# A two-layer threshold-attention and squared-ReLU kernel: the order of its first loads, of its PSUM banks, and of its side work at the seams

## The chip, the cores and the metric

The kernel runs on one core of one Trainium2 chip. The metric is the device time of one execution in microseconds: the median of 3 runs of the kernel before is 1271.97 us (1270.42 to 1272.17). Five engines work beside each other: TensorE (PE, with PEld for its weight loads), VectorE (DVE), ScalarE (ACT), GpSimd (POOL) and SyncE (SP), which here only issues DMAs. Each runs its own instructions in the order in which they were written, and waits for the others by semaphores.

## The reference

All arithmetic is float32. The weights of the two layers come in as 64-bit floats and are converted on the chip.

```python
# q, k, v: (8, 8, 576, 64); w_in: (512, 2048); w_out: (2048, 512)
scores = scale * np.matmul(q, k.transpose(0, 1, 3, 2))
thresh = np.max(scores, axis=-1, keepdims=True) - tau
scores = np.where(scores >= thresh, scores, -1000000000.0)
attn = np.exp(scores - np.max(scores, axis=-1, keepdims=True))
attn = attn / (np.sum(attn, axis=-1, keepdims=True) + 1e-09)
x = np.matmul(attn, v)          # -> (4608 tokens, 512), heads side by side
h = np.maximum(x @ w_in, 0.0)
out = (h * h) @ w_out
```

## The kernel before

The program has three stages, one behind the other. **Attention** takes pairs of heads; `load_q` and `load_k` bring queries and keys, `turn` transposes them on PE against the identity `ident` into PSUM and evicts them scaled by `qscale` (made from `tau`), `scores` multiplies, DVE and ACT do the softmax, `values` multiplies by v. Its PSUM is one tile `sc` of six banks and a pool `pt` of two. At the start, `keep_busy` runs transposes of the identity on PE while the first loads are under way. `rn` is a tile that holds the last 64 queries of both heads and the last 64 keys' chunk; `load_k` fills it by small loads.

The two layers are matrix products done by Strassen's scheme in Winograd's form, twice nested: seven outer products m, in the order `OUTER` = 1, 2, 6, 7, 4, 5, 3, each made of seven inner products k, in the order 1, 6, 7, 5, 2, 4, 3. The **hidden layer** (first layer) runs over all tokens first. The **output layer** (second layer) then runs over nine steps n of 512 tokens, 49 products of eight matmuls each per step.

`inner` is one outer product m. Its banks are called X, Y, Z, W here. PE makes X (k = 1), Y (k = 6), Z (k = 7), W (k = 5), then adds onto X (k = 2), Z (k = 4) and W (k = 3). ACT copies X out as p1 (`copy`, the **first copy**, line 813); DVE adds u2 = Y + p1 and u3 = Z + u2, and `final` takes each of the four results out (line 126). Z may be added to again only when u3 has read it. Between these, `tick(0)` to `tick(6)` call `also`, which issues side work.

The **side work** of the output layer makes the operands of products that come later. `inner_sums(n, m)` makes, for the next m, its operands k = 5, 6 and 3 on POOL and its operand k = 7 on DVE. The latter is `sum_v`: ACT copies one input into a PSUM tile `c` of the pool `b` (two buffers, line 857), then DVE subtracts (line 123). `outer_sums` makes operands of another m, all in that manner. `spread` deals the list of side work over the seven ticks. With the four items of `inner_sums` alone, the fourth (k = 7) falls on tick 6. The lists of i = 4 and 5 (m = 4 and 5) have ten items in steps 0 to 7, of which two fall on tick 6; that of i = 6 (m = 3) has eight. In step 0, i = 0, 1 and 2 have longer lists, too.

```python
for w in work[n * at // 7 : n * (at + 1) // 7]:
    w()
```

The order of every engine's instructions is the order of these calls: the whole is scheduled by hand.

Of the kernel before, what the change touches and what calls it, by code (L numbers as in the profile page):

```python
# [10 lines left out]
FP32 = mybir.dt.float32  # L11
I32 = mybir.dt.int32
U32 = mybir.dt.uint32
ALU = mybir.AluOpType
# [34 lines left out]
def kernel(  # L49
# [54 lines left out]
    sb, cv = Region(arena, 0, X_AT[0]), Region(arena, X_AT[0], ARENA)  # L104

    ident = const.tile([P, P], FP32, name="ident")
    make_identity(nc, ident)

    tau_c = const.tile([P, 1], FP32, name="tau_c")

# [14 lines left out]
    def plus(e, out, x, y):  # L125
        e.tensor_tensor(out=out, in0=x, in1=y, op=ALU.add)  # L126
# [184 lines left out]
    def load_k(i):  # L311
        b, hp = pairs[i]
        h = 2 * hp
        kn = sb.tile([P, FULL, P], FP32, tag="kn", bufs=2, name="kn")
        rn = sb.tile([P, P], FP32, tag="rn", bufs=2, name="rn")
        loaded[i, 1], loaded[i, 2] = kn, rn
        for j in range(2):
            queue = nc.scalar if i == 0 and j == 0 else nc.sync
            keys = k[b, h + j, :, :].rearrange("(p c) d -> p c d", c=CH)
            for e in range(2):  # L320
                yield queue.dma_start(
                    out=kn[ds(e * HALF, HALF), :, ds(j * D, D)],
                    in_=keys[:, ds(e * FULL, FULL), :],
                )
            if i == 0 and j == 0:
                wide = bass.AP(tensor=tau.tensor, offset=tau.offset, ap=[[0, P], [1, 1]])
                nc.scalar.dma_start(out=tau_c[:, :], in_=wide)
            yield queue.dma_start(out=rn[REST:P, ds(j * D, D)], in_=keys[:, CH - 1, :])
        yield nc.sync.dma_start(
            out=rn[0:REST, :].rearrange("p (j d) -> p j d", j=2),  # L330
            in_=q[b, h : h + 2, MAIN:S, :].rearrange("j p d -> p j d"),
        )
# [81 lines left out]
    def turn(i, which, spots, other=None):  # L414

        while any(x[0:2] == (i, which) for x in wanted):
            ahead(1)
        nat, to = loaded.pop((i, which)), places(i)
        of = [nat[:, t, :] for t in range(FULL)] + ([loaded.pop((i, 2))] if which else [])
        for t, x in enumerate(of):  # L420
            for r, (spot, at) in enumerate(spots):
                rows = ds(r * HALF, HALF)
                made = nc.tensor.transpose(spot[:, ts(t, HALF)], x[rows, :], ident[rows, rows])  # L423
                touch("turns", made, at, BANK)
        half, kind = FULL * HALF, "turnedk" if which else "turnedq"

        def scaled(to, spot):
            touch(kind, nc.scalar.activation(out=to, in_=spot[0], func=AF.Identity, scale=qscale[:, :]), spot[1], BANK, i)

        def then():  # L430
            part = lambda r, x, n: (spots[r][0][:, ds(x, n)], spots[r][1])
            if which:
                for r, n in ((0, half), (1, half + REST)):
                    spot = part(r, 0, n)
                    copy_by = other if r and other else nc.scalar.copy
                    touch(kind, copy_by(to[1][:, ds(r * half, n)], spot[0]), spot[1], BANK, i)
                scaled(to[2], part(0, half, REST))
                ask_ahead(i, 1)
            else:
                for r in range(2):  # L440
                    scaled(to[0][:, ds(r * half, half)], part(r, 0, half))
                ask_ahead(i, 0)

        return then
# [330 lines left out]
        for name in BEGIN_WITH.get(p) or (CONVERTING if converts(p) else PLAIN):  # L775
            step(name.rstrip("-"), p - name.count("-"))

    def inner(product, copy, temp, bank, final, tick):

        X = bank()
        product(X, 1, False)
        p1 = temp("p1")
        copy(p1, X)
        tick(0)
        Y = bank()
        product(Y, 6, False)
        u2 = temp("u2")  # L790
        plus(nc.vector, u2, Y, p1)
        tick(1)
        Z = bank()
        product(Z, 7, False)
        u3 = temp("u3")
        plus(nc.vector, u3, Z, u2)
        tick(2)
        W = bank()
        product(W, 5, False)
        final((1, 1), W, u3)  # L800
        tick(3)
        product(X, 2, True)
        final((0, 0), X, None)
        tick(4)
        product(Z, 4, True)
        final((1, 0), Z, u2)
        tick(5)
        product(W, 3, True)
        final((0, 1), W, u2)
        tick(6)  # L810
# [151 lines left out]

    hid = Region(arena, 0, 26 * BANK)
    squares, clock = deque(), {"n": 0}
    def hidden_bank():
        return banks.tile([P, BANK], FP32, tag="b", bufs=6, name="ph")

    def square(n, j, o):
# [90 lines left out]
    fin = Region(arena, 0, 0)  # L1059
    fin.ring("gi", XB[0:6])  # L1060
    fin.ring("u", [XB[6], XI, XI + BANK])
    fin.ring("t", [13 * BANK + P * i for i in range(4)] + [XI + 2 * BANK + P * i for i in range(4)])
    fin.ring("t3", [XI + 3 * BANK + 3 * P * i for i in range(3)])
    fin.ring("o", [0, 2 * BANK])
    KINDS = (1, 2, 7, 4, 5, 6, 3)
# [45 lines left out]
    def output_layer(n, also):  # L1111
        bank = lambda: banks.tile([P, BANK], FP32, tag="b", bufs=6, name="po")[:, 0:P]
        temp = lambda name: fin.tile([P, P], FP32, tag="t")
        AT = {(0, 0): 0, (1, 1): 1, (1, 0): 2, (0, 1): 3}
        U2 = fin.tile([P, 4, P], FP32, tag="u")
        U3 = fin.tile([P, 4, P], FP32, tag="u")
        o = {}

        def give_out(row, ab, queue):

            a, b = ab
            to = out[ds(n * STEP + row * 2 * NQ + a * NQ, NQ), :].rearrange("p (c b o) -> p c b o", c=2, b=2)
            if queue is None:
                later.append((to[:, :, b, :], o[row][:, :, AT[ab], :]))
            else:
                queue.dma_start(out=to[:, :, b, :], in_=o[row][:, :, AT[ab], :])

        for m in OUTER:
            where = {2: (0, 0), 4: (1, 0), 5: (1, 1), 3: (0, 1)}.get(m)
            if where and where[0] not in o:  # L1130
                o[where[0]] = fin.tile([P, 2, 4, P], FP32, tag="o")
            mine = U3 if m in (4, 5) else U2
            t3 = fin.tile([P, 3, P], FP32, tag="t3") if m != 1 else None

            at_end = n == NSTEP - 1 and m == OUTER[-1]

            def product(to, k, more):
                g, w = operands[n, m, k], W_OUT[m, k].rearrange("p (k o) -> p k o", k=4)
                for j in range(4):
                    by_tiles(to, g[:, j, :], w[:, j, :], not more and j == 0, j == 3)  # L1140

            def sums_to(i, e, c):

                if where:
                    plus(e, o[where[0]][:, where[1], i, :], c, mine[:, i, :])
                if m in (5, 6):
                    plus(e, U2[:, i, :], c, U2[:, i, :])
                if m == 7:
                    plus(e, U3[:, i, :], c, U2[:, i, :])

            def final(ab, c, other):
                i = AT[ab]
                if m == 1 and other is None:
                    nc.scalar.copy(U2[:, i, :], c)
                elif m == 1:
                    plus(nc.vector, U2[:, i, :], c, other)
                elif other is None:
                    sums_to(i, nc.vector, c)
                else:
                    plus(nc.vector, t3[:, i - 1, :], c, other)  # L1160
                    if at_end:
                        sums_to(i, nc.vector, t3[:, i - 1, :])
                if at_end:
                    give_out(0, ab, nc.sync if i % 2 else nc.scalar)

            inner(product, copy, temp, bank, final, lambda at: also(m, at))
            if m != 1 and not at_end:
                sums_to(slice(1, 4), nc.gpsimd, t3[:, :, :])
            if m in (5, 3) and not at_end:
                for ab in AT:  # L1170
                    give_out(where[0], ab, None)
# [8 lines left out]
    with tc.manual_schedule():  # L1180
        with ExitStack() as stack:
# [3 lines left out]
            def keep_busy(times, to=None):  # L1185
# [3 lines left out]
                for _ in range(times):  # L1189
                    nc.tensor.transpose(to, ident[:, :], ident[:, :])  # L1190

            for _ in load_q(0):
                pass
            for _ in load_k(0):
# [4 lines left out]
            ask_ahead(0, 0)  # L1199
            ask_ahead(0, 1)  # L1200
            ahead(99)
            keep_busy(15)
            pq = pt_pool.tile([P, 2, BANK], FP32, tag="pt", name="pq")
            turn(0, 0, [(pq[:, r, :], None) for r in range(2)])()
            keep_busy(8, sc[:, ds(5 * BANK, P)])
            turn(0, 1, spots(), nc.vector.tensor_copy)()
            for p in range(FIRST_PERIOD, NU // 2 + 6):
                run_period(p)
# [6 lines left out]
            for _ in range(60):  # L1215
                sums_step()
            ask()
        b_pool = ctx.enter_context(tc.tile_pool(name="b", bufs=2, space=PSUM))
        banks = ctx.enter_context(tc.tile_pool(name="banks", bufs=1, space=PSUM))

        def reload(at):

# [195 lines left out]
```

## Time and profile before

| what | value |
|---|---|
| median of 3 runs | 1271.97 us |
| profiled execution, first to last instruction | 1273.4 us |
| attention, to the first product of the first layer | 0 to 494.7 us |
| first layer | 494.8 to 882.5 us |
| second layer's products | 882.6 to 1269.5 us |
| PE busy in the span | 1251.7 us (98%) |
| DVE, ACT, POOL busy in the span | 988.2, 844.3, 982.5 us (78%, 66%, 77%) |
| mean granted TensorE clock | 0.996 |

The profile is of one execution; it gives its span, which is 1.4 us above the median of the runs, so a sum made against the profile is carried over to the median as a difference. PE is the engine to watch: where it idles in the layers, the time grows by as much.

### The profile page before, as it was taken

How to read it: one execution, taken by the hardware profiler on the slowest of the kernel's cores; microseconds unless marked ns; L12 is line 12 of the kernel's file. 1: busy time of each engine (PE TensorE's matmuls, PEld its weight loads, DVE VectorE, ACT ScalarE, POOL GpSimd, SP SyncE). 2: the span in 40 equal slices, each digit the busy share in tenths (PEclk: the TensorE clock that was granted, in tenths of full speed). 3: DMA queues.
4: the chain of work that ended last, by engine and by line, in shares of the span. 5: the costliest groups of instructions: out<-in, count | busy, mean ns of one | idle time of the engine just before them, and what ended most of it. 6: DMA issues, size and time to landing. Idle time of an engine off the chain costs nothing.

```text
span 1273.4 us, 55161 instructions
## 1 busy us (share of the span) xinstructions
PE 1251.7 (98%) x22991; PEld 1093.6 (86%) x22991; DVE 988.2 (78%) x2385; ACT 844.3 (66%) x1536; POOL 982.5 (77%) x1070
## 2 busy tenths in 40 slices
PE   8999999999999999999999999999999999999998
PEld 5777776777777778988888888999999999999998
DVE  6999998999999996886887878867746654665463
ACT  6999998999999994666765856675524432443240
POOL 2999998877776542988898989868787878787776
PEclk8999999999999999999999999999999999999999
DMA  7566677434333323657667657579965336533511
GB/s 186 143 161 154 167 198 188 120 89 107 89 81 89 83 53 97 192 166 237 202 191 231 215 169 249 172 274 369 267 163 152 83 107 163 146 84 107 167 35 35
DMA packets 289912, 196.79 MB, mean 155 GB/s; under 512 B 98560, under 2 KB 250624, under 8 KB 289664
## 3 DMA queue, kind: packets, MB, share of 16 engines
q1 hardware_dynamic: 288352, 192.86, 52.8%
q8 instruction: 181, 2.97, 1.0%
q14 instruction: 67, 0.55, 0.1%
q10 hardware_dynamic: 1312, 0.41, 0.1%
HBM read 120.85 MB, written 72.35 MB: 152 GB/s over the span
## 4 chain that ended last, share of the span: by engine, by line
PE 72%; DMA 3%; ACT 2%; POOL 2%; DVE 1%; issue 1%; DVEq 0%; ACTq 0%; POOLq 0%; SPq 0%
PE po L818 27%; PE ph L997 17%; PE ph L818 10%; PE sc L561 7%; PE sc L459 6%; PE pt L403 4%; PE sc L542 1%; PE sc L423 1%; POOL arena L126 1%; DMA g<-arena 1%; ACT arena L970 1%; DVE arena L126 1%; DMA w<-arena 1%; ACT arena L971 1%; ACT c L857 1%
## 5 line engine op out<-in xcount | busy, mean ns | idle before, releaser
L126 POOL TENSOR_TENSOR arena<-arena 128x512 f32<-128x512 f32 (+1 forms) x314 | 378.7, 1224 | 125.1 <-DVE arena L126 113.5
L818 PE MATMUL po<-wall,arena 128*64 128x128 f32 x7056 | 385.8, 273 | 1.4 <-ACT arena L813 0.8
L818 PEld LDWEIGHTS po<-wall,arena 128*64 128x64 f32 x7056 | 385.1, 137 | 1.9 <-ACT arena L813 1.0
L126 DVE TENSOR_TENSOR arena<-ph,arena 128x512 f32<-128x512 f32 x378 | 254.5, 688 | 77.4 <-PE ph L997 30.9
L123 POOL TENSOR_TENSOR arena<-arena 128x128 f32<-128x128 f32 (+1 forms) x322 | 265.5, 826 | 24.1 <-DMA arena<-w 8.5
L997 PE MATMUL ph<-arena,wall 128*128 128x256 f32 x1176 | 256.7, 380 | 2.3 <-DVE arena L126 2.1
L997 PEld LDWEIGHTS ph<-arena,wall 128*128 128x128 f32 x1176 | 222.4, 190 | 36.3 <-DVE arena L126 6.2
L126 DVE TENSOR_TENSOR arena<-po,arena 128x128 f32<-128x128 f32 x378 | 107.6, 288 | 159.3 <-PE po L818 151.4
L492 DVE SCALAR_TENSOR_TENSOR arena<-arena 128x576 f32<-128x576 f32 x288 | 225.9, 820 | 0.4 <-ACT arena L487 0.3
L487 ACT ACTIVATE arena<-arena 128x576 f32<-128x576 f32 x288 | 214.1, 781 | 13.4 <-DVE arena L477 13.3
L477 DVE TENSOR_SCALAR_CACHE_REDUCE arena<-sc 128x576 f32<-128x576 f32 x288 | 203.4, 752 | 18.5 <-ACT arena L552 5.7
L857 ACT COPY c<-arena 128x512 f32<-128x512 f32 (+1 forms) x295 | 168.9, 578 | 70.1 <-DVE arena L123 36.1
L459 PE MATMUL sc<-arena 64*64 64x512 f32 (+1 forms) x2304 | 179.6, 415 | 5.6 <-ACT arena L552 1.2
L561 PE MATMUL sc<-arena 64*64 64x128 f32 (+1 forms) x5760 | 165.6, 261 | 1.0 <-ACT arena L552 0.5
L123 DVE TENSOR_TENSOR arena<-arena,c 128x512 f32<-128x512 f32 x235 | 154.2, 664 | 12.1 <-ACT c L857 7.1
L561 PEld LDWEIGHTS sc<-arena 64*64 64x64 f32 x5760 | 150.4, 133 | 4.5 <-ACT arena L552 0.7
L552 ACT COPY arena<-pt 128x1024 f32<-128x1024 f32 x143 | 145.0, 1014 | 4.6 <-PE pt L403 3.9
L459 PEld LDWEIGHTS sc<-arena 64*64 64x64 f32 x2304 | 76.8, 134 | 71.4 <-issue 47.2
L813 ACT COPY arena<-po 128x128 f32<-128x128 f32 x63 | 16.6, 264 | 177.6 <-PE po L818 174.8
L818 PE MATMUL ph<-arena,wall 128*64 128x128 f32 x2352 | 129.2, 273 | 0.6 <-DVE arena L710 0.6
L818 PEld LDWEIGHTS ph<-arena,wall 128*64 128x64 f32 x2352 | 128.3, 137 | 1.4 <-issue 1.0
L484 POOL TENSOR_SCALAR arena<-arena,tau_p 128x2 f32<-128x2 f32 x144 | 83.8, 582 | 58.5 <-DVE arena L477 44.7
(55 smaller groups left out, 1142.5 us busy)
## 6 DMA issues: line engine op xcount, KB each, us to landing
gp<-arena SPq DMA_DIRECT2D x96, 256.0 KB, 3.4
arena<-gp SPq DMA_DIRECT2D x96, 256.0 KB, 5.4
w<-arena SPq DMA_DIRECT2D x60, 256.0 KB, 2.7
wall<-w SPq DMA_DIRECT2D x49, 256.0 KB, 5.3
g<-arena SPq DMA_DIRECT2D x48, 256.0 KB, 3.7
arena<-g SPq DMA_DIRECT2D x48, 256.0 KB, 5.0
arena<-w SPq DMA_DIRECT2D x44, 256.0 KB, 3.4
arena<-in_v_dram SPq DMA_DIRECT2D x32, 288.0 KB, 3.8
```

The costliest lines, as they stand in the source:

```text
L123: e.tensor_tensor(out=out, in0=x, in1=y, op=ALU.subtract)
L126: e.tensor_tensor(out=out, in0=x, in1=y, op=ALU.add)
L459: made = nc.tensor.matmul(sc[at, ds(to, count)], lhs, kT[rows, ds(at_k, count)], start=True, stop=True)
L477: made = nc.vector.tensor_scalar(out=s[:, j, :], in0=sc[:, ds(at, S)], scalar1=1.0, scalar2=None, op0=ALU.mult, op1=ALU.min, accum_out=nmx ...
L484: nc.gpsimd.tensor_scalar(out=thr, in0=nmx, scalar1=tau_p[:, :], scalar2=None, op0=ALU.add)
L487: nc.scalar.activation(out=w[:, :, j, :], in_=of(j), func=AF.Exp, bias=nmx[:, j : j + 1], scale=-1.0)
L492: nc.vector.scalar_tensor_tensor(out=w[:, :, j, :], in0=of(j), scalar=thr[:, j : j + 1], in1=w[:, :, j, :], op0=ALU.is_le, op1=ALU.mult, a ...
L552: touch(kind, copy_by(joined(to), whole(pt, 0, count)), at, 2 * BANK, m)
L561: made = nc.tensor.matmul(sc[ds(u * D, D), ds(5 * j * BANK + row, count)], loaded_v[i][rows, (c - (u != j)) % CH, :], wT[m][rows, ds(weigh ...
L818: nc.tensor.matmul(to[cols], lhs[:, cols], rhs, start=start, stop=stop, skip_group_check=True)
L857: nc.scalar.copy(c, y)
L997: nc.tensor.matmul(to[:, 2 * j : 2 * j + 2, :], W_IN[m, k][:, ts(2 * h + j, P)], part_x(steps, k, m), start=(not more and j == 0), stop=Tr ...
```

## The change

1. The identity is made inside the schedule, ahead of the first loads. The load of `tau` goes first on ACT's queue. For the first pair, one load on POOL's queue replaces the two small loads of `rn`'s keys (one on ACT's, one on SP's), and the load of `rn`'s queries moves from SP to ACT.
2. `keep_busy` runs 12 and 3 transposes where it ran 15 and 8, and the second half of the first query eviction goes from ACT to DVE.
3. The pools of the layers are opened in the other order, so that `banks` lies on the first six banks and `b` on the two that `pt` had; the first two products of the first layer take their banks from `b`.
4. The ring of small temporaries `t` of the second layer starts at its other half.
5. In the second layer, what `also` does at tick 6 of each m but the last is put off to tick 0 of the next m, behind that m's first copy.
6. In the very last m, POOL adds what is known beforehand, so that DVE has one addition less behind each of three results.

Lines of the changed kernel are higher by 16 in this part: its first copy is at line 829, the side copy at 873, and the two helpers for sums at 122 and 125 (before 813, 857, 123 and 126).

```diff
     ident = const.tile([P, P], FP32, name="ident")
-    make_identity(nc, ident)
...
         loaded[i, 1], loaded[i, 2] = kn, rn
+        first = i == 0
+        if first:
+            wide = bass.AP(tensor=tau.tensor, offset=tau.offset, ap=[[0, P], [1, 1]])
+            nc.scalar.dma_start(out=tau_c[:, :], in_=wide)
         for j in range(2):
-            queue = nc.scalar if i == 0 and j == 0 else nc.sync
+            queue = nc.scalar if first and j == 0 else nc.sync
...
-            if i == 0 and j == 0:
-                wide = bass.AP(tensor=tau.tensor, offset=tau.offset, ap=[[0, P], [1, 1]])
-                nc.scalar.dma_start(out=tau_c[:, :], in_=wide)
-            yield queue.dma_start(out=rn[REST:P, ds(j * D, D)], in_=keys[:, CH - 1, :])
-        yield nc.sync.dma_start(
+            if not first:
+                yield queue.dma_start(out=rn[REST:P, ds(j * D, D)], in_=keys[:, CH - 1, :])
+        queue = nc.scalar if first else nc.sync
+        if first:
+            yield nc.gpsimd.dma_start(
+                out=rn[REST:P, :].rearrange("p (j d) -> p j d", j=2),
+                in_=k[b, h : h + 2, :, :].rearrange("j (p c) d -> p j c d", c=CH)[:, :, CH - 1, :],
+            )
+        yield queue.dma_start(
             out=rn[0:REST, :].rearrange("p (j d) -> p j d", j=2),
...
                 for r in range(2):
-                    scaled(to[0][:, ds(r * half, half)], part(r, 0, half))
+                    into, spot = to[0][:, ds(r * half, half)], part(r, 0, half)
+                    if r and other:
+                        made = nc.vector.tensor_scalar(
+                            out=into, in0=spot[0], scalar1=qscale[:, :], scalar2=None, op0=ALU.mult
+                        )
...
         plus(nc.vector, u2, Y, p1)
+        ready(((1, 0), (0, 1)), u2)
...
         plus(nc.vector, u3, Z, u2)
+        ready(((1, 1),), u3)
...
+    begun_in = [2]
+
     def hidden_bank():
+        if begun_in[0]:
+            begun_in[0] -= 1
+            return b_pool.tile([P, BANK], FP32, tag="b", name="c")
         return banks.tile([P, BANK], FP32, tag="b", bufs=6, name="ph")
...
-    fin.ring("t", [13 * BANK + P * i for i in range(4)] + [XI + 2 * BANK + P * i for i in range(4)])
+    fin.ring("t", [XI + 2 * BANK + P * i for i in range(4)] + [13 * BANK + P * i for i in range(4)])
...
+                elif at_end:
+                    plus(nc.vector, o[0][:, where[1], i, :], c, t3[:, i - 1, :])
                 else:
                     plus(nc.vector, t3[:, i - 1, :], c, other)
-                    if at_end:
-                        sums_to(i, nc.vector, t3[:, i - 1, :])
...
-            inner(product, copy, temp, bank, final, lambda at: also(m, at))
+            def ready(blocks, c):
+
+                for ab in blocks if at_end else ():
+                    plus(nc.gpsimd, t3[:, AT[ab] - 1, :], c, mine[:, AT[ab], :])
+
+            def tick(at, m=m):
+
+                if at == 6 and m != OUTER[-1]:
+                    put_off.append(lambda: also(m, at))
+                    return
+                while put_off:
+                    put_off.pop()()
+                also(m, at)
+
+            inner(product, copy, temp, bank, final, tick, ready)
...
+            make_identity(nc, ident)
             for _ in load_q(0):
...
-            keep_busy(15)
+            keep_busy(12)
...
-            turn(0, 0, [(pq[:, r, :], None) for r in range(2)])()
-            keep_busy(8, sc[:, ds(5 * BANK, P)])
+            turn(0, 0, [(pq[:, r, :], None) for r in range(2)], nc.vector)()
+            keep_busy(3, sc[:, ds(5 * BANK, P)])
...
+        banks = ctx.enter_context(tc.tile_pool(name="banks", bufs=1, space=PSUM))
         b_pool = ctx.enter_context(tc.tile_pool(name="b", bufs=2, space=PSUM))
-        banks = ctx.enter_context(tc.tile_pool(name="banks", bufs=1, space=PSUM))
```

ACT's rows in the last step n = 8 of the second layer, from the first copy of m = 2 to that of m = 4. `po` are banks of the second layer's products, `c` the side copy's PSUM tiles; the numbers tell the tiles apart. Before:

```order
L813 COPY arena_167<-po_19289 128x128
L857 COPY c_19359<-arena_167 128x512
L813 COPY arena_167<-po_19363 128x128
L857 COPY c_19433<-arena_167 128x512
L813 COPY arena_167<-po_19437 128x128
L857 COPY c_19507<-arena_167 128x512
L813 COPY arena_167<-po_19511 128x128
```

After, from the side copy that now follows m = 2's first copy:

```order
L829 COPY arena_167<-po_19277 128x128
L873 COPY c_19287<-arena_167 128x512
L829 COPY arena_167<-po_19351 128x128
L873 COPY c_19361<-arena_167 128x512
L829 COPY arena_167<-po_19425 128x128
L873 COPY c_19435<-arena_167 128x512
```

The two pieces read alike, but the pairing has moved by one. Before, `c_19359` behind m = 2's first copy (`po_19289`) is for m = 6. After, `c_19287` behind m = 2's first copy (`po_19277`) is for m = 2 itself. DVE's rows at that place are in the same order in both kernels: after, its subtraction that reads `c_19287` stands ahead of m = 2's u2:

```order
L122 TENSOR_TENSOR arena_167<-arena_167,c_19287 128x512
L125 TENSOR_TENSOR arena_167<-po_19290,arena_167 128x128
L125 TENSOR_TENSOR arena_167<-po_19301,arena_167 128x128
L125 TENSOR_TENSOR arena_167<-po_19311,arena_167 128x128
L125 TENSOR_TENSOR arena_167<-po_19277,arena_167 128x128
```

The first row makes operand k = 7, which PE loads for its third product, Z (`po_19301`).

PE's rows where attention ends and the first layer begins (`L561` and `L575` are the last products with v), before:

```order
L561 MATMUL sc<-arena 64x128 x2
L561 MATMUL sc<-arena 64x64 x4
L818 MATMUL ph<-arena,wall 64x128 x392
L997 MATMUL ph<-arena,wall 128x256 x588
L818 MATMUL ph<-arena,wall 64x128 x784
```

All 392 matmuls of the first pass go to the banks `ph` there. After, at the same place:

```order
L575 MATMUL sc<-arena 64x128 x2
L575 MATMUL sc<-arena 64x64 x4
L834 MATMUL c<-arena,wall 64x128 x16
L834 MATMUL ph<-arena,wall 64x128 x16
L834 MATMUL c<-arena,wall 64x128 x8
L834 MATMUL ph<-arena,wall 64x128 x352
```

The first two products of eight matmuls each, and the later addition onto the first, now go to banks of the pool `b`.

More of the change, by code (lines that the diff above doesn't have):

```diff
@@ L440, in then @@
                 for r in range(2):
-                    scaled(to[0][:, ds(r * half, half)], part(r, 0, half))
+                    into, spot = to[0][:, ds(r * half, half)], part(r, 0, half)
[3 more added lines that the diff above has]
+                        )
+                        touch(kind, made, spot[1], BANK, i)
+                    else:
+                        scaled(into, spot)
                 ask_ahead(i, 0)
@@ L776, in run_period, with inner @@
             step(name.rstrip("-"), p - name.count("-"))
-    def inner(product, copy, temp, bank, final, tick):
+    def inner(product, copy, temp, bank, final, tick, ready=lambda blocks, c: None):
         X = bank()
@@ L1116, in output_layer @@
         U3 = fin.tile([P, 4, P], FP32, tag="u")
-        o = {}
+        o, put_off = {}, []
         def give_out(row, ab, queue):
```

## The prediction

> **What bounds the kernel now.** First the page: its span, and its chain of work that ended last, by engine and by line.
>
> ```profile
> span 1273.4 us, 55161 instructions
> PE 72%; DMA 3%; ACT 2%; POOL 2%; DVE 1%; issue 1%; DVEq 0%; ACTq 0%; POOLq 0%; SPq 0%
> PE po L818 27%; PE ph L997 17%; PE ph L818 10%; PE sc L561 7%; PE sc L459 6%; PE pt L403 4%; PE sc L542 1%; PE sc L423 1%; POOL arena L126 1%; DMA g<-arena 1%; ACT arena L970 1%; DVE arena L126 1%; DMA w<-arena 1%; ACT arena L971 1%; ACT c L857 1%
> ```
>
> TensorE carries 72% of the chain, and the second layer's products (`po`) alone 27%. The groups of instructions of the stretch from 883 us to the end show how tightly TensorE is packed there:
>
> ```profile
> L818 PE MATMUL po<-wall,arena 128*64 128x128 f32 x7052 | 385.6, 273 | 1.4 <-ACT arena L813 0.8 <-DVE arena L126 0.6
> ```
>
> It idles 1.4 us in 385.6. A step has 49 products, nine steps 441, so one product takes 385.6/441 = 0.874 us; I call that a beat. No edit to this layer's order can win more than those 1.4 us and the tail, and every new wait of TensorE adds its full length. So the question is what the put-off side work makes TensorE wait for. The timeline of an ordinary seam between two m (DVE and ACT):
>
> ```profile
> 1068.31 0.68 DVE L123 TENSOR_TENSOR arena<-arena,c 128x512 f32<-128x512 f32 x1
> 1068.97 0.27 ACT L813 COPY arena<-po 128x128 f32<-128x128 f32 x1 [5.35 <-PE po L818]
> 1069.13 0.60 ACT L857 COPY c<-arena 128x512 f32<-128x512 f32 x1
> ...
> 1074.21 0.29 DVE L126 TENSOR_TENSOR arena<-po,arena 128x128 f32<-128x128 f32 x1 [0.58 <-PE po L818]
> 1074.42 0.68 DVE L123 TENSOR_TENSOR arena<-arena,c 128x512 f32<-128x512 f32 x1
> ...
> 1075.09 0.27 ACT L813 COPY arena<-po 128x128 f32<-128x128 f32 x1 [5.36 <-PE po L818]
> 1075.25 0.60 ACT L857 COPY c<-arena 128x512 f32<-128x512 f32 x1
> ```
>
> Read it from the bottom. X of the new m ends just ahead of its first copy at 1075.09, so Y ends a beat later, near 1075.9, and Z begins then. Z loads operand k = 7. DVE made that operand at 1074.42 to 1075.10, directly behind the old m's last result (1074.21). It could, because ACT's side copy for it had run at 1069.13, behind the old m's own first copy, five microseconds ahead of its use. That early copy is the cover. The 0.8 us or so between 1075.10 and Z are the slack.
>
> **The change part by part.** *Side work behind the next first copy, ordinary seams.* After the change the side copy for k = 7 stands behind the new m's first copy, in ACT's queue, and DVE's subtraction and u2 stand behind it in turn. The first copy cannot leave 1075.09, since it waits for X. What is queued behind it: one side copy, then on DVE the subtraction, u2 and u3; on TensorE, Z and all that follows. The durations are in the rows above; the two hand-overs are here, ACT to DVE in the first two rows, DVE to TensorE in the last two:
>
> ```profile
> 882.13 0.58 ACT L857 COPY c<-arena 128x512 f32<-128x512 f32 x1
> 882.75 0.69 DVE L126 TENSOR_TENSOR arena<-arena,c 128x512 f32<-128x512 f32 x1 [0.93 <-ACT c L857]
> ...
> 925.14 0.28 DVE L126 TENSOR_TENSOR arena<-po,arena 128x128 f32<-128x128 f32 x1
> 925.48 1.62 PEld L818 LDWEIGHTS po<-wall,arena 128*64 128x64 f32 x30 [0.85 <-DVE arena L126]
> 925.48 1.75 PE L818 MATMUL po<-wall,arena 128*64 128x128 f32 x28 [0.60 <-DVE arena L126]
> ```
>
> Each takes about 0.05 us. So at this seam: first copy 1075.09; side copy from 1075.25, ended 1075.85; subtraction from 1075.90, ended 1076.58; Z's first weights from 1076.63. Where the instruction waits for two semaphores a separate wait is queued ahead of it, which I put at 0.1 us for both engines together: 1076.73. When would Z have begun? X's last record ends 0.05 ahead of the first copy, at 1075.04, Y's at 1075.91. A record lasts 0.273 us while 16 of them make a beat, one every 0.055, so the next product's first weights go in about 0.27 before the last record ends: 1075.64. The delay is 1076.73 - 1075.64 = 1.1 us; it would be 0.8 if Z began only where Y's last record ends, and 1.2 with slower hand-overs. The rows at 925.48 show the same difference in small: the weight loads idled 0.85, the pipelined products 0.60, and it is the former that counts.
>
> How many such seams? With four items the fourth, k = 7, falls on tick 6. That is so for i = 0 to 3 in steps 1 to 7 (28 seams), i = 3 in step 0 (1; there i = 0 to 2 have longer lists, in which k = 7 falls on tick 3), and i = 0 to 5 in step 8 (6). Together 35 seams, 35 x 1.1 = 38.5 us, from 28 to 42.
>
> *The same, seams with more side work.* At the seams into m = 5 and m = 3 of steps 0 to 7, two side subtractions for the next step are put off. Z does not need them, but DVE does them ahead of u2. The timeline around m = 3:
>
> ```profile
> 1038.41 0.27 ACT L813 COPY arena<-po 128x128 f32<-128x128 f32 x1 [5.36 <-PE po L818]
> ...
> 1050.52 0.28 DVE L126 TENSOR_TENSOR arena<-po,arena 128x128 f32<-128x128 f32 x1
> 1050.72 2.02 DVE L123 TENSOR_TENSOR arena<-arena,c 128x512 f32<-128x512 f32 x3
> 1051.16 0.26 ACT L813 COPY arena<-po 128x128 f32<-128x128 f32 x1
> ...
> 1052.66 0.28 DVE L126 TENSOR_TENSOR arena<-po,arena 128x128 f32<-128x128 f32 x1
> ...
> 1053.45 0.28 DVE L126 TENSOR_TENSOR arena<-po,arena 128x128 f32<-128x128 f32 x1
> ```
>
> DVE runs three side subtractions between the old m's last result (1050.52) and u2 (1052.66); u3 ends at 1053.73. X of m = 3 ends 14 beats after the first copy at 1038.41, so its own could start at 1050.65, where before it stood behind side copies until 1051.16. TensorE adds onto Z four beats after X, near 1054.1, its weights 0.27 earlier, 1053.83, and must have u3 by then: 0.05 us of slack. (The wait at 925.48 above is this one in step 0, where there is none left.) After the change: first copy 1050.65, side copies ended 1051.40 and 1051.99, subtractions ended 1052.12 and 1052.72. The third copy needs a buffer that is free at 1052.12, ends 1052.74, its subtraction ends 1053.46, u2 runs to 1053.7, one more subtraction to 1054.3, u3 to 1054.5. That is 0.7 us late, at eight seams 5.6 us; between nothing, if the third copy finds a buffer, and 1.3 each (10 us), the whole of two subtractions. Into m = 5 only two subtractions stand ahead of u2, u3 comes about 0.7 late into about as much slack: nothing. The three long lists of step 0 put off operands that are needed a whole m later: nothing.
>
> *The start.* TensorE's rows, the last load issued for the first pair, and the times to landing of the two small loads:
>
> ```profile
> 4.43 0.60 SPq L329 DMA_DIRECT2D arena<-in_q_dram  x1
> ...
> 4.86 0.69 PE L423 MATMUL pq<-ident,arena 64*128 64x64 f32 x8
> 5.48 1.97 PE L1190 MATMUL sc<-ident 128*128 128x128 f32 x8
> 7.38 0.52 PE L423 MATMUL sc<-ident,arena 64*128 64x64 f32 x10
> ```
> ```profile
> arena<-in_q_dram SPq DMA_DIRECT2D x1, 32.0 KB, 2.1
> arena<-in_k_dram ACTq DMA_DIRECT2D x1, 16.0 KB, 3.1
> ```
>
> The keys' transposes at 7.38 stand behind eight busy transposes of 0.246 us; the last load landed at 4.43 + 2.1 = 6.5. With three busy transposes, and loads that go out earlier on three queues, they start near 6.0: 1.4 us earlier. `tau` first and DVE's share of the eviction keep the queries off that path. The identity is POOL's first work in both kernels: nothing. POOL's load has no row before. At 3.1 us from 1.3, when the identity is done, it lands at 4.4 and is hidden; at twice that, 7.5, it costs 0.1; and no gain or up to 1 us of loss is possible if fewer busy transposes leave TensorE slow for longer. I take -1.4, between -1.8 and +1.
>
> *The other seams and the tail.* The rows of the two seams and of the last instruction:
>
> ```profile
> 494.77 5.46 PE L818 MATMUL ph<-arena,wall 128*64 128x128 f32 x96 [0.57 <-DVE arena L710]
> 887.02 5.24 PE L818 MATMUL po<-wall,arena 128*64 128x128 f32 x92 [0.77 <-ACT arena L813]
> 1270.16 0.29 DVE L126 TENSOR_TENSOR arena<-arena 128x128 f32<-128x128 f32 x1
> ```
>
> The first layer no longer waits for the last reader of attention's banks: -0.5 of 0.57. The first copy at 887 waited on its place in the ring `t`; with the other half first: -0.8. DVE's second addition at the end goes: -0.3; POOL's three additions that replace it need u2 and u3, which are ready some beats earlier. Each could be nothing.
>
> *The sum.* 38.5 + 5.6 - 1.4 - 0.5 - 0.8 - 0.3 = 41.1 us. The span, 1273.4, would become 1314.5; the median of the runs, 1272.0, becomes **1313 us**.
>
> **The rivals.** *Faster: the first copies are what hurts.* If side work ahead of the first copy delayed TensorE and Z did not need the late subtraction, the change gains. For it speaks that the first copy does come late before (1051.16 for 1050.65). Against it: TensorE idled only 1.4 us, and the first copy is needed four beats after X begins. Its place is the addition onto X; it decides if operand k = 7 is made elsewhere in time. Price: all of the gains above and the other wait, -3.0 - 0.6, so 1268 us. Chance 4%.
>
> *Slower still: TensorE's clock.* New pauses may lower the granted clock. Rows of the trace by stretch, with TensorE's busy time first and the granted clock third from the end:
>
> ```profile
> 205.30:208.80 3.50, 2.09 (x58) 1.72 (x54) 2.72 (x9) 2.43 (x7) 3.26 (x5) 1.00 0.53 138
> 208.80:212.20 3.40, 3.40 (x46) 1.93 (x40) 1.47 (x5) 1.51 (x3) 0.61 (x1) 0.50 0.68 188
> 602.00:606.00 4.00, 2.21 (x11) 1.59 (x10) 2.21 (x4) 1.18 (x2) 3.09 (x6) 1.00 0.67 238
> 606.00:610.00 4.00, 4.00 (x20) 3.54 (x20) 3.23 (x6) 2.10 (x5) 1.95 (x3) 1.00 0.63 202
> ```
>
> In attention, a stretch with 2.09 of 3.50 us busy (60%) was followed by 3.4 us at half clock. In the first layer, 2.21 of 4.00 (55%) was not. A second-layer stretch of 3.4 us around a pause of 1.1 would be 68% busy. If each of the 35 pauses brought one such half-clock stretch, each would cost half of 3.4, 1.7 us: 60 us more, 1373; if one in three did, 1333. The layer's own row speaks against it. The Trainium skill (TensorE: Matmul & The Clock Gate, Part 1) says that half clock returns after an idle window of about 3.4 us; by that, no pause here would touch the clock and the sum stands at 1313. The trace's row at 205.30 differs from it, since TensorE was busy for 2.09 us of that stretch, so I keep the rival. Chance 6%.
>
> *Milder: the pause is only where records end.* If hand-overs overlap and the pause is 0.8 or less, 28 us, and u3 finds a buffer, the time is 1272 + 28 - 3 = 1297. Chance 8%.
>
> **How the numbers follow.** The forecast, 35 pauses near 1.1 us, gets 82%. Its bounds: low, 35 x 0.9 with no late u3 and 3.5 of gains, 1300; high, 35 x 1.2 with 10 for u3 and no gains, 1324. The rivals outside hold 18%, so 1300 to 1324 is the range. Faster by over 0.2% (2.5 us, about what a measurement of this kernel can tell from no change): 4%, the first rival; within it: 2%, where pauses would have to cancel the gains; slower: 94%.
>
> **What would show it.** Right: among the waits, some 35 waits of `po`'s weight loads for DVE's subtraction of a side copy, each near 1.1 us in the weight loads; DVE's subtraction waiting for ACT's side copy as often; the second layer longer by some 43 us, all else shorter by 2 to 3; the keys' transposes near 6.0 us; the granted clock unchanged from 883 us on. Wrong: `po`'s idle time still near 1 us, or half clock in the second layer, or pauses at only the eight long seams.

## The result, and the profile after

The changed kernel takes 1312.41 us (median of 5 runs, 1309.73 to 1315.2), the kernel before 1270.99 us (median of 5, 1269.9 to 1272.17). The ratio is 1.0329, with a 95% interval of 1.0314 to 1.0345: slower by 40 to 44 us. The profiled execution spans 1310.4 us for 1273.4.

The page of the changed kernel, span and chain that ended last, by engine and by line:

```profile
span 1310.4 us, 55126 instructions
PE 68%; ACT 5%; DVE 4%; issue 2%; POOL 1%; DMA 1%; DVEq 0%; SPq 0%; ACTq 0%; POOLq 0%
PE po L834 23%; PE ph L1018 17%; PE ph L834 9%; PE sc L575 7%; PE sc L473 6%; PE pt L410 3%; DVE arena L122 3%; ACT c L873 3%; PE sc L556 1%; DVE arena L125 1%; PE sc L430 1%; ACT arena L991 1%; ACT arena L992 1%; POOL arena L125 1%; DMA arena<-gp 1%
```

ACT and DVE have gone from 2% and 1% to 5% and 4%, and two lines have come up to 3% each: the side copy (`ACT c L873`, 1% before by its old line 857) and DVE's subtraction that reads it (`DVE arena L122`), which stood on no line of the chain before. The second layer's products by their line, with first and last start, before and after:

```profile
L818 PE MATMUL po<-wall,arena x7056: 272/273/324, 882.6 to 1269.5; 128*64 128x128 f32 x196
```
```profile
L834 PE MATMUL po<-wall,arena x7056: 272/273/324, 878.2 to 1306.5; 128*64 128x128 f32 x196
```

The second layer has grown from 386.9 to 428.3 us, by 41.4; all that comes ahead of it is 4.4 us shorter in this pair of profiles, which is mostly not the change's doing (below). A matmul still takes 273 ns. The groups of instructions from 878 us on say what TensorE waited for:

```profile
L834 PE MATMUL po<-wall,arena 128*64 128x128 f32 x7056 | 395.1, 273 | 33.4 <-DVE arena L122 29.1 <-DVE arena L125 3.5 <-PE po L834 0.8
L834 PEld LDWEIGHTS po<-wall,arena 128*64 128x64 f32 x7056 | 385.4, 137 | 43.0 <-PE po L834 37.3 <-DVE arena L125 5.7
```

Among the waits, the weight loads' 37.3 us are 35 waits, the longest 1.1 us. (They are put down to PE there, whose wait they take over; the products' own row names DVE's subtraction for 34 of them.) An ordinary seam on the timeline, to be laid beside the rows at 1074.21 to 1075.25 of before:

```profile
984.34 0.29 DVE L125 TENSOR_TENSOR arena<-po,arena 128x128 f32<-128x128 f32 x1 [0.58 <-PE po L834]
985.21 0.27 ACT L829 COPY arena<-po 128x128 f32<-128x128 f32 x1 [6.43 <-PE po L834]
985.37 0.60 ACT L873 COPY c<-arena 128x512 f32<-128x512 f32 x1
986.07 0.69 DVE L122 TENSOR_TENSOR arena<-arena,c 128x512 f32<-128x512 f32 x1 [1.44 <-ACT c L873]
986.68 0.28 DVE L125 TENSOR_TENSOR arena<-po,arena 128x128 f32<-128x128 f32 x1
986.87 1.76 PEld L834 LDWEIGHTS po<-wall,arena 128*64 128x64 f32 x32 [1.07 <-PE po L834]
986.90 1.86 PE L834 MATMUL po<-wall,arena 128*64 128x128 f32 x30 [0.86 <-DVE arena L122]
```

ACT stood idle for 6.43 us with the side copy behind a first copy that could not start. DVE's subtraction, which before followed the old m's last result without a wait, now waits 1.44 us for ACT, and Z begins 0.11 us after it has ended. And the seam into m = 3, with three subtractions ahead of u2:

```profile
1013.05 1.11 ACT L873 COPY c<-arena 128x512 f32<-128x512 f32 x2
...
1013.68 2.03 DVE L122 TENSOR_TENSOR arena<-arena,c 128x512 f32<-128x512 f32 x3 [0.26 <-ACT c L873]
1014.40 1.19 ACT L873 COPY c<-arena 128x512 f32<-128x512 f32 x2 [0.24 <-DVE arena L122]
1015.63 0.28 DVE L125 TENSOR_TENSOR arena<-po,arena 128x128 f32<-128x128 f32 x1
...
1016.42 0.28 DVE L125 TENSOR_TENSOR arena<-po,arena 128x128 f32<-128x128 f32 x1
...
1016.76 2.38 PEld L834 LDWEIGHTS po<-wall,arena 128*64 128x64 f32 x43 [0.66 <-DVE arena L125]
```

The third copy (the first of the pair at 1014.40) starts when DVE's first subtraction has freed a buffer; u3 ends at 1016.70, and the addition onto Z has waited 0.66 us for it. The granted clock from 925 us on (each row: the stretch, its length, the busy time of TensorE and of the other engines, and third from the end the clock):

```profile
925.00:1100.00 175.00, 160.04 (x2860) 155.91 (x2858) 86.48 (x229) 49.98 (x106) 122.20 (x103) 1.00 0.43 116
1100.00:1306.00 206.00, 188.94 (x3377) 184.13 (x3374) 103.79 (x274) 59.09 (x125) 141.43 (x121) 1.00 0.30 87
```

No half clock there: the rival of the clock is out.

### The profile page after: what moved, and what is told of

Same layout as the page of the kernel before. It is cut to its first block, busy times and chain, and to the rows that moved or that the text cites. A ratio compares the mean times of both kernels' runs of the same rounds, so it can differ in the third digit from the quotient of the medians.

```text
span 1310.4 us, 55126 instructions
## 1 busy us (share of the span) xinstructions
PE 1259.9 (96%) x22983; PEld 1092.4 (83%) x22983; DVE 988.3 (75%) x2383; ACT 843.2 (64%) x1535; POOL 983.2 (75%) x1074
## 4 chain that ended last, share of the span: by engine, by line
PE 68%; ACT 5%; DVE 4%; issue 2%; POOL 1%; DMA 1%; DVEq 0%; SPq 0%; ACTq 0%; POOLq 0%
PE po L834 23%; PE ph L1018 17%; PE ph L834 9%; PE sc L575 7%; PE sc L473 6%; PE pt L410 3%; DVE arena L122 3%; ACT c L873 3%; PE sc L556 1%; DVE arena L125 1%; PE sc L430 1%; ACT arena L991 1%; ACT arena L992 1%; POOL arena L125 1%; DMA arena<-gp 1%
## 5 line engine op out<-in xcount | busy, mean ns | idle before, releaser
L125 POOL TENSOR_TENSOR arena<-arena 128x512 f32<-128x512 f32 (+2 forms) x317 | 379.5, 1215 | 165.2 <-DVE arena L125 147.9
L834 PE MATMUL po<-wall,arena 128*64 128x128 f32 x7056 | 395.1, 273 | 33.4 <-DVE arena L122 29.1
L834 PEld LDWEIGHTS po<-wall,arena 128*64 128x64 f32 x7056 | 385.4, 137 | 43.0 <-PE po L834 37.3
L122 POOL TENSOR_TENSOR arena<-arena 128x128 f32<-128x128 f32 (+1 forms) x322 | 265.2, 825 | 24.2 <-DMA arena<-w 7.6
L873 ACT COPY c<-arena 128x512 f32<-128x512 f32 (+1 forms) x295 | 167.9, 579 | 68.1 <-DVE arena L122 39.6
L122 DVE TENSOR_TENSOR arena<-arena,c 128x512 f32<-128x512 f32 x235 | 154.7, 667 | 70.1 <-ACT c L873 67.4
L575 PE MATMUL sc<-arena 64*64 64x128 f32 (+1 forms) x5760 | 166.3, 261 | 0.9 <-ACT arena L566 0.5
L575 PEld LDWEIGHTS sc<-arena 64*64 64x64 f32 x5760 | 150.7, 133 | 4.6 <-issue 1.0
L834 PE MATMUL ph<-arena,wall 128*64 128x128 f32 x2304 | 126.5, 273 | 0.1
```

The lines of the kernel that those rows point to most:

```text
L122: e.tensor_tensor(out=out, in0=x, in1=y, op=ALU.subtract)
L575: made = nc.tensor.matmul(sc[ds(u * D, D), ds(5 * j * BANK + row, count)], loaded_v[i][rows, (c - (u != j)) % CH, :], wT[m][rows, ds(weigh ...
L834: nc.tensor.matmul(to[cols], lhs[:, cols], rhs, start=start, stop=stop, skip_group_check=True)
L873: nc.scalar.copy(c, y)
```

## The experiments

The theory: the put-off alone makes the loss, because the side copy for operand k = 7 is queued behind a first copy that waits for TensorE. The rivals are that other edits carry part of it, that any side work behind the first copy would cost, and, for the start, that the loads and not the clock set it. Each run is compared with runs of the kernel before on its own chip.

**Without the put-off, all other edits kept.**

```diff
             def tick(at, m=m):
-                if at == 6 and m != OUTER[-1]:
-                    put_off.append(lambda: also(m, at))
-                    return
-                while put_off:
-                    put_off.pop()()
                 also(m, at)
```

> The changed kernel with the side work of tick 6 given out at tick 6 again; all other edits stay. Theory (late operand: the put-off alone makes the pauses, 35 of 1.08 us and eight of 0.6 us): 1312.4 - 42.6 = 1269.8 us, between 1268 and 1271.5, and TensorE idles under 1 us in the second layer's products. Rival (the other edits carry part of the loss, for example through the exchanged banks or the ring of temporaries): above 1275 us, with pauses left in the second layer.

Measured: 1272.5 us against 1272.07, ratio 1.0007 (0.9993 to 1.0021). The group of the second layer's products:

```profile
L834 PE MATMUL po<-wall,arena 128*64 128x128 f32 x7056 | 385.8, 273 | 0.6 <-ACT arena L829 0.5
```

The loss is gone and so is all idle time but 0.6 us: the rival falls. But 1272.5 lies above the 1268 to 1271.5 that were expected: the other edits together win nothing that can be measured.

**The put-off alone, on the kernel before.** The same lines, added to the kernel before.

> The kernel before with the put-off alone. Theory (late operand): 1271.0 + 42.6 = 1313.6 us, between 1311 and 1317, with 35 pauses of about 0.86 us and eight of about 0.42 us in the pipelined products. Rival (it needs the other edits beside it): under 1300 us.

Measured: 1313.75 us against 1272.07, ratio 1.0334 (1.0314 to 1.0353). Its products' group:

```profile
L818 PE MATMUL po<-wall,arena 128*64 128x128 f32 x7056 | 395.1, 273 | 34.0 <-DVE arena L123 29.1 <-DVE arena L126 3.3 <-PE po L818 0.8
```

This is the changed kernel's row over again. The put-off is both needed and enough.

**Put-off kept, operand k = 7 made earlier.** In the lists of four the order becomes 5, 7, 6, 3.

```diff
...
-                work = [] if i == 6 else inner_sums(n, OUTER[i + 1])
+                short = i < 6 and not (n == 0 and i < 3) and not (more and i > 3)
+                work = [] if i == 6 else inner_sums(n, OUTER[i + 1], (5, 7, 6, 3) if short else (5, 6, 3, 7))
...
```

> The changed kernel, put-off and all, but in the lists of four items the sums are dealt in the order k = 5, 7, 6, 3, so that k = 7 is made at tick 3 and it is k = 3, used seventh, that is put off. Theory (late operand): the 35 pauses vanish and the eight at the long seams stay, 1312.4 - 37.8 = 1274.6 us, between 1272 and 1277. Rival (the put-off as such costs: any side work behind the first copy holds the seam up): 1308 us or more.

Measured: 1277.67 us against 1272.07, ratio 1.0045 (1.0030 to 1.0061). The products' group, and DVE's subtractions:

```profile
L834 PE MATMUL po<-wall,arena 128*64 128x128 f32 x7056 | 387.9, 273 | 4.6 <-DVE arena L125 4.6
L122 DVE TENSOR_TENSOR arena<-arena,c 128x512 f32<-128x512 f32 x167 | 111.8, 682 | 17.5 <-POOL arena L125 12.0 <-ACT c L873 3.2
```

All waits for the subtraction (29.1 us in the products' row) are gone; the eight waits for u3 are left. So the put-off as such is harmless at ordinary seams, and what is put off must not be due at once. The time is just past the 1277 expected: the eight waits sum to 4.6 us here, for 3.5 in the changed kernel, and DVE's subtractions now wait 12.0 us for POOL (1.2 in the changed kernel), in whose queue the put-off sum (k = 3) now stands later. Whether the one makes the other longer was not tried.

**Put-off at the long seams alone.**

```diff
-                if at == 6 and m != OUTER[-1]:
+                if at == 6 and m in (4, 5) and n < NSTEP - 1:
```

> The changed kernel with the put-off kept only behind m = 4 and m = 5 of steps 0 to 7, the seams with ten items. Theory (late operand): no pause at ordinary seams, eight of about 0.42 us (0.6 us of delay) at m = 3: 1269.8 + 4.8 = 1274.6 us, between 1272.5 and 1277. Rival (the eight pauses at m = 3 come from lateness that the 35 others bring along): as without any put-off, 1268 to 1271.5 us, and no pause at m = 3.

Measured: 1275.89 us against 1272.07, ratio 1.0036 (1.0021 to 1.0050). The products' group:

```profile
L834 PE MATMUL po<-wall,arena 128*64 128x128 f32 x7056 | 387.4, 273 | 3.9 <-DVE arena L125 3.4 <-ACT arena L829 0.5
```

Eight waits for u3, 3.4 us in the products' row, one to a step and each at m = 3, none at m = 5: the lateness is made at that seam and does not come from the 35 others. The second layer lasts 391.1 us (877.8 to 1268.9) for 386.1 (877.9 to 1264.0) without any put-off, so each costs 5.0/8 = 0.62 us.

**The side copy twice at the 35 ordinary seams.** `sum_v` repeats its copy there.

```diff
...
-        nc.scalar.copy(c, y)
+        for _ in range(times):
+            nc.scalar.copy(c, y)
...
```

> The changed kernel, put-off and all, with ACT's side copy for k = 7 done twice at the 35 ordinary seams. Theory (the chain first copy, side copy, subtraction, third product sets each pause): every pause grows by one copy, 0.55 to 0.6 us, so 35 x 0.58 = 20 us more than the changed kernel, 1331 to 1334 us. Rival (the pause is set elsewhere, by DVE's order or by POOL's sums, and the side copy is hidden): under 1318 us.

Measured: 1333.48 us against 1270.95, ratio 1.0492 (1.0478 to 1.0507): 21 us above the changed kernel. One seam, and the clock of the stretches around it:

```profile
988.16 0.27 ACT L829 COPY arena<-po 128x128 f32<-128x128 f32 x1 [6.43 <-PE po L834]
988.32 1.22 ACT L874 COPY c<-arena 128x512 f32<-128x512 f32 x2
989.64 0.69 DVE L122 TENSOR_TENSOR arena<-arena,c 128x512 f32<-128x512 f32 x1 [2.06 <-ACT c L874]
...
990.45 0.66 PEld L834 LDWEIGHTS po<-wall,arena 128*64 128x64 f32 x12 [1.70 <-issue]
990.48 0.77 PE L834 MATMUL po<-wall,arena 128*64 128x128 f32 x10 [1.48 <-DVE arena L122]
```
```profile
986.00:990.00 4.00, 2.99 (x56) 2.75 (x51) 0.94 (x3) 1.35 (x3) 2.27 (x3) 1.00 0.99 259
990.00:994.00 4.00, 3.52 (x65) 3.55 (x67) 1.41 (x5) 0.00 (x0) 2.49 (x2) 1.00 0.50 122
```

One copy more, 0.62 us, and the pause grows from 1.07 to 1.70. The copy lies on the path at its full length. Even pauses of this size leave the clock at 1.00.

**The start: busy transposes as before, loads on three queues.** On the kernel without the put-off, `keep_busy(12)` and `keep_busy(3, ...)` go back to 15 and 8.

> The changed kernel without the put-off, with 15 and 8 busy transposes at the start as before; the loads on three queues stay. Theory (clock: with 12 and 3, TensorE is not busy enough to leave half clock before the first scores, which then take 4 us for 2): the first scores run at full clock in about 2.2 us, and the first softmax instruction begins at 9.3 to 10.1 us, where it was 10.1 to 10.6 with 12 and 3. Rival (loads: the keys land late because more queues only share the same DMA engines): the keys' transposes wait for a load past 7.4 us and the softmax begins no earlier than 10.1 us. The total stays within 0.3% of the kernel before by both.

Measured: 1269.46 us against 1270.95, ratio 0.9991 (0.9982 to 1.0000). TensorE's timeline of the changed kernel, and of this one:

```profile
1.35 2.82 PE L1225 MATMUL idle<-ident 128*128 128x128 f32 x12 [1.35 <-POOL ident masks.py:199]
4.96 0.69 PE L430 MATMUL pq<-ident,arena 64*128 64x64 f32 x8 [0.79 <-DMA arena<-in_q_dram]
5.58 0.90 PE L1225 MATMUL sc<-ident 128*128 128x128 f32 x3
6.41 0.98 PE L430 MATMUL sc<-ident,arena 64*128 64x64 f32 x10
8.07 4.12 PE L473 MATMUL sc<-arena 64*64 64x512 f32 x32 [0.68 <-ACT arena L435]
```
```profile
6.92 0.53 PE L430 MATMUL sc<-ident,arena 64*128 64x64 f32 x10
8.15 2.18 PE L473 MATMUL sc<-arena 64*64 64x512 f32 x32 [0.70 <-ACT arena L435]
```

With 12 and 3, TensorE begins the scores 0.08 us sooner and needs 4.12 us for what takes 2.18 with 15 and 8. The first softmax instruction began at 10.61 us in the changed kernel and at 9.60 here, as the theory of the clock had it. That TensorE was slow is read off these durations: the granted clock reads 1.00 from 8 to 12 us in both profiles. (In the run with k = 7 earlier, whose start is that of the changed kernel, it reads 0.50 from 8.02 to 11.42 us, with the scores at 3.86 us.) With the start as before, the softmax began at 10.06 in the profile of before, but at 9.27 in that of the put-off alone and at 9.13 and 9.06 in those of the last two runs below, so the loads on three queues won nothing that shows.

**The start: gaps filled.** Sixteen transposes, three, and four more between the keys' transposes and the scores.

> The changed kernel without the put-off, with 16 busy transposes ahead of the queries, 3 behind them and 4 more between the keys' transposes and the first scores, so that TensorE is busy without a gap from 1.3 us on. Theory (clock): full clock by about 8.2 us whatever the phase of the clock's windows, first softmax instruction at 8.9 to 9.9 us, total 0 to 1.5 us under the kernel before. Rival (loads): keys' transposes still wait for a load near 6.5 to 7 us, softmax at 10.1 us or later.

Measured: 1271.4 us against 1270.95, ratio 1.0002 (0.9984 to 1.0021), where 0 to 1.5 us under the kernel before had been expected. The scores took 2.18 us, as with 15 and 8, and the first softmax instruction began at 9.81 us. But the keys' transposes waited for a load until 6.59, as the rival had it (its softmax at 10.1 us or later did not come), and DVE's eviction then waited 1.11 us for the four transposes. Nothing is won over 15 and 8.

**The start as before, the edits of the seams and the tail alone.**

> The kernel before with the bank order, the first layer's beginning in the pool b, the ring of temporaries and POOL's additions at the end, with the start as before and no put-off. Theory (the two seams and the tail are worth what their pauses were, and the start is worth nothing): 0.5 + 0.8 + 0.3 us at most, so 0.1% under the kernel before, and neither the 0.57 us pause ahead of the first layer nor the 0.77 us pause at the head of the second is left. Rival (they are made up by later waits): both pauses gone and the layers as long as before.

Measured: 1270.68 us against 1270.95, ratio 0.9990 (0.9980 to 1.0000). The pause ahead of the first layer and the one at the head of the second are gone, and one of 0.5 us has come: a first copy late behind side work, at m = 2 of step 0. So of the 0.8 us at the second layer's head most comes back as a later wait, as the rival had it; the run without the put-off has the same pause.

**That one seam.** The put-off is added to the kernel of the last run for m = 1 of step 0 alone.

```diff
+                if at == 6 and n == 0 and m == OUTER[0]:
```

> The kernel before with the edits of the seams and the tail and the start as before, and the put-off at one seam alone, the one from m = 1 to m = 2 in step 0, where without the put-off the first copy stands behind side work and TensorE pauses for 0.55 us. Theory (the put-off pays only where the first copy itself is late and the work behind it is not due at once): that pause goes, TensorE idles under 0.2 us in the second layer's products, and the time is 0.1 to 0.2% under the kernel before. Rival (DVE's later side work makes u3 late there instead): a pause of 0.3 to 0.6 us at that m, and the time as without any put-off.

Measured: 1270.79 us against 1270.71, ratio 0.9992 (0.9982 to 1.0003). Its products' group:

```profile
L827 PE MATMUL po<-wall,arena 128*64 128x128 f32 x7056 | 385.8, 273 | 0.1
```

TensorE idles 0.1 us in the whole second layer. At this seam the put-off does what it can do, and that is worth less than a measurement can tell: 0.1 to 0.2% had been expected, 0.08% was measured, and the interval includes 1. No version that was run is faster than the kernel before beyond its interval.

## Why the prediction was right

**The 35 ordinary seams: right.** 1.1 us each and 38.5 in all were forecast; the weight loads' row shows 37.3 us in 35 waits, 1.07 each. The put-off alone reproduced it, making k = 7 earlier took it away, and doubling the copy lengthened it by one copy. That the weight loads' idle time and not the products' is what counts is borne out, too: the rows say 1.07 and 0.86, and the second layer has grown by 41.4 us, which the 33.4 us of the products' row (35 x 0.86 and eight of 0.42) would not make. The hand-overs from ACT to DVE to TensorE, put at 0.2 us in all with the queued waits, are 0.10 us (from 985.97 to 986.07) and 0.11 us (from 986.76 to 986.87) in the rows.

**The eight long seams: right.** 5.6 us were forecast, 0.7 each; 0.62 each, 5.0 in all, were measured. The buffer that the third copy was to wait for is the one it waits for in the trace. No pause at m = 5, as forecast.

**The start: wrong.** It was to give 1.4 us back. The keys' transposes did begin earlier, at 6.41 us for 7.38 (6.0 was forecast), but the first softmax instruction came later, at 10.61 for 10.06. Three steps failed. The first is the starting point. The 7.38 us stood behind eight busy transposes of 0.246 us, and that was their slow speed in that one profile: with the start as before, they took 1.09 to 1.18 us in three others for the 1.97 there, and the keys' transposes began at 6.59 (put-off alone), 6.01 (start as before) and 6.29 us (one seam). The second of these:

```profile
4.99 1.09 PE L1213 MATMUL sc<-ident 128*128 128x128 f32 x8
6.01 0.46 PE L423 MATMUL sc<-ident,arena 64*128 64x64 f32 x8
```

So in these profiles 0.8 to 1.4 us of it came without any change to the start. The second step: loads that go out earlier did not land earlier. The views of the issued loads in the first 9 us, after:

```profile
2.61 0.87 ACTq L336 DMA_DIRECT2D arena<-in_q_dram  x1
```
```profile
arena<-in_k_dram POOLq DMA_DIRECT2D x1, 32.0 KB, 4.1
arena<-in_q_dram ACTq DMA_DIRECT2D x1, 32.0 KB, 4.1
```

The last load goes out at 2.61 for 4.43 and lands after 4.1 us for 2.1, so at 6.7 for 6.5. The third step: the scores ran at about half speed (4.12 us for 2.18) for want of busy transposes. The forecast took their durations for granted and kept a slow TensorE as no more than an end of the range. The Trainium skill (TensorE: Matmul & The Clock Gate, Part 1) has full clock after about 3.4 us of sustained activity, in windows that run free of the kernel. Here the scores at 8.07 us were still slow 6.7 us after the first transpose, with 0.79 us without work between, which agrees with "sustained". But that gap is not shown to be the reason. In the run with k = 7 earlier, whose start is the same, the queries' transposes were fast right behind such a gap (0.47 us for 0.69), and the scores were slow again:

```profile
4.96 0.47 PE L430 MATMUL pq<-ident,arena 64*128 64x64 f32 x8 [0.79 <-DMA arena<-in_q_dram]
7.75 3.86 PE L473 MATMUL sc<-arena 64*64 64x512 f32 x32 [0.68 <-ACT arena L435]
```

With 12 and 3, full speed was had there and lost again as the scores began: TensorE was busy for 1.89 of the 3.50 us from 4.5 to 8.0 us, and the granted clock was 0.50 from 8.02 to 11.42 us.

**The other seams and the tail: half right.** TensorE's first product of the first layer now starts without a wait:

```profile
491.73 1.97 PE L834 MATMUL c<-arena,wall 128*64 128x128 f32 x32
```

The 0.5 us are there. So are the 0.8 at the second layer's head, but without the put-off a pause of 0.5 comes at m = 2. At the end, DVE's last addition is done at 1307.1, 3.3 us ahead of the span's end; before, it was 1270.45 and 3.0. From the last matmul's start to the end it is 3.9 us in both; over all eleven profiles it is 3.9 and 4.1 us with the old tail and 3.6 to 4.2 with the new one, so the 0.3 us that DVE won do not show beyond the scatter. So of 3.0 us of gains little remained: the gross loss, forecast at 44.1, was 37.3 + 5.0 = 42.3, and the medians differ by 41.4 (40 to 44 by the interval). Two errors of about 2 us each, a loss too large and gains too large, nearly cancel. That the total came within 1 us of 1313 is luck to that extent; the path of the loss is not.

**The clock: rightly set aside.** With 43 pauses, and with 35 longer ones in the run with two copies, it stayed at 1.00. The rule of the Trainium skill (TensorE: Matmul & The Clock Gate, Part 1), that half clock returns after an idle window of about 3.4 us, agrees with the second layer, where the longest pause was 1.7 us.

**The profile's own difference** is 37.0 us for 41.4 between medians. Before, the first layer had one wait of 1.78 us (at 605.00) that the profile after lacks; the run of the one seam, which does not touch that place, has 1.9 us there again. The first layer's first product started between 490.67 and 494.80 us over all eleven profiles. Both look like scatter of single executions and were not pursued.

## What to carry to other kernels

Work that is dealt over slots has a due time: before it is moved behind an instruction that waits for another engine, ask for every item when its result is used. An engine that looks idle may be held up by the first instruction of its queue: here a copy whose input was ready stood behind one whose input was not, and moving it by that one place cost 1.07 us thirty-five times. And where transposes only keep TensorE busy, their number sets how fast TensorE runs afterwards, and is not padding to be trimmed to the arrival of the data. A gap read off one profile may hold a duration that the next profile does not have: the eight busy transposes took 1.97 us in one and 1.09 in another.

## What the runs showed that was not expected

- Twelve and three busy transposes left TensorE slow for the first scores: 3.86 to 4.12 us in all five profiles with them, 2.18 in all six with more. The granted clock shows it in one of the five only; in the others it reads 1.00 there.
- Spread over three queues, the first pair's last load landed at 6.7 us for 6.5; POOL's own load of 32 KB took 4.1 us, as long as ACT's of the same size.
- TensorE 55% to 75% busy in 4 us stretches of the layers kept full clock (2.21 and 2.99 of 4.00 us), while 60% in a stretch of attention, and 54% at the start of the run with k = 7 earlier (1.89 of 3.50 us), were followed by 3.4 us at half clock. What tells them apart was not tried.
